# Attention and a rational feed-forward layer: eight of twelve weight conversions moved from the attention's time into the first whole chunk

## The chip, the core and the metric

The kernel runs on one core of a Trainium2 chip. The metric is the device time of one execution in microseconds; lower is better. The engines of the core are PE (matrix products; PEld is its weight load), DVE (vector), ACT (scalar and activation functions), POOL (the third elementwise engine) and SP, whose queue issues almost all DMAs of this kernel. Each engine takes its instructions in the order in which they stand.

## The reference, cut to what matters

```python
def _attn_ref(q, k, v):            # 8 batches, 8 heads, 576 positions, 64 wide
    scores = scale * np.matmul(q, k.transpose(0, 1, 3, 2))
    mask = block_i >= block_j      # blocks of 64 positions
    scores = np.where(mask, scores, -1000000000.0)
    attn = softmax(scores)
    return np.matmul(attn, v)
...
def _moe_ref(x, w_in, w_out, a, b):   # x: 4608 tokens x 512; d_ff = 2048
    h = x @ w_in
    P = a[0] + a[1] * h + a[2] * h2 + a[3] * h3
    Q = 1.0 + np.abs(b[0]) * np.abs(h) + np.abs(b[1]) * h2
    g = P / (Q + 1e-06)
    return g @ w_out
```

The attention's output, heads side by side, is x. The softmax is written out in the reference. The two weight matrices come as 64-bit floats.

## The kernel before, in words

**Precision.** Products are made with pairs of a high and a low part: a matrix product is three matmuls (high with high, high with low, low with high). A weight tile is therefore converted before use: the 64-bit words are put together into a 32-bit float, which is then split into a high part and a remainder.

**Blocks and steps.** d_ff is cut into 16 blocks of 128. Two blocks have four tiles of 128 x 2 x 512: two of w_in and two of w_out. One tile is one conversion step (`Weights.convert`, L142 to L181, a generator that makes a step each time it is asked): a load of 512 KB on SP (L153), an absolute value with scaling on ACT (L164), a shift on DVE (L165), two combined shift-or operations on DVE (L166, L168), a copy to the high part on ACT (L172 or L177), and a subtraction for the low part on POOL (L173 or L178). For the first ten blocks the raw words are loaded into the very tile that later holds the two parts, and the working tile `ab` of the shift lies in PSUM. For the last six blocks, whose weight tiles have no room in SBUF while the attention runs, the step takes its buffers from the rings `os`, `u`, `v` and `s` of the feed-forward units, works in SBUF throughout (`ab` is `at`), and stores the two parts in a scratch tensor in DRAM (L180, two DMAs of 256 KB). These are twelve steps; they are spread over attention steps 80 to 230 (WB0, WBN).

**The attention** takes 32 pairs of heads, ten small steps each: scores (L513, L530), maximum (L548), exponential (L560), division (L569, L572), transposes (L598) and the product with v (L648, L664). A pair's output is split into xh and xl and stored to `xscr`; half of xh is first copied across the partitions by a DMA into xt (L668), added to xl on POOL (L671), and xl is then stored (L672).

**The feed-forward layer** works in units, of two blocks by 256 tokens in the first phase and one block by 512 tokens in the second. A unit has a first product (`first`, L229), whose result h goes through ACT, POOL and DVE (L236 to L245), a reciprocal by logarithm and exponential with a correction (`recip`, L251 to L269), a split into gh and gl (`split`, L277 and L278), and a second product (`second`, L299). The three stages run one, two and three units behind the first. The first phase computes the first ten blocks for 14 chunks of 256 tokens while the attention runs, and stores partial sums to `pscr` (L310). The second phase begins with a whole chunk (chunk 7: all 16 blocks, 16 units, of which the first ten need only the blocks that are there), goes on with seven chunks that add the last six blocks to the partial sums, and ends with another whole chunk. A chunk's x is loaded from `xscr` in four tiles (L214).

**At the change of phase** (L752 to L764) the attention's pools are given back, and the tiles of the last six blocks, the pool `ffb` and further PSUM buffers are opened in their place. Then the rest of the units is emitted in half-steps n = 0, 1, 2 ...; from n = 4 (WF) on, each half-step also issues one reload of a converted tile from the scratch tensor (L761, 512 KB), twelve in all.

A scheduler then sets the order on each engine from the program and its own model of times; the order that is written is not the order that runs.

Of the kernel before, what the change touches and what calls it, by code (L numbers as in the profile page):

```python
# [8 lines left out]
F32 = mybir.dt.float32  # L9
# [24 lines left out]
KQB = 3  # L34
XB = 3
WR, WF = 1, 4
HOLD = 4
ALAG3 = 10
OFFS = (0,3,5)
# [11 lines left out]
NFA = 10  # L51
NFB = NF - NFA
# [8 lines left out]
def units_of(ph, c):  # L61
    return NFA // NBU[0] if ph == 0 else NFB if c < NSP else NF
# [11 lines left out]
def attn_ffn_kernel(  # L74
# [16 lines left out]
    ffn = ctx.enter_context(tc.tile_pool(name="ffn", bufs=2))  # L91
    ps_h = ctx.enter_context(tc.tile_pool(name="ps_h", bufs=1, space=PSUM))
# [27 lines left out]
    class Weights:  # L120
# [19 lines left out]
        def wout(self, f, y):  # L140
            return self.tile(("o", f, 0))[:, y]

        def convert(self):
            last = []
            for key in self.places:
                x, f, d = key
                f += self.f0
                src = w_in[d * 128:(d + 2) * 128, f * 128:(f + 2) * 128] if x == "i" else w_out[f * 128:f * 128 + 128]
                nm = f"{x}{f}_{d}"
                there = self.dt is F32R  # L150
# [7 lines left out]
                                      reason="order")  # L158
                words = raw.rearrange("p a f -> p (a f)").rearrange("p (f t) -> p f t", t=2)
                w0, w1 = words[:, :, 0], words[:, :, 1]  # L160
                at = ffn.tile([128, 512], F32, name=f"wa{nm}", tag="u")
                ab = ps_h.tile([128, 512], F32, name=f"wc{nm}", tag="a") if there else at
                ai, bi = at.bitcast(I32), ab.bitcast(I32)
                nc.scalar.activation(out=ab, in_=w1.bitcast(F32), func=AF.Abs, scale=WSCALE)  # L164
                nc.vector.tensor_scalar(out=bi, in0=bi, scalar1=3, scalar2=None, op0=ALU.logical_shift_left)  # L165
# [8 lines left out]
                else:  # L174
                    bt = ffn.tile([128, 512], F32R, name=f"wb{nm}", tag="v")
                    pt = ffn.tile([128, 512], F32R, name=f"wp{nm}", tag="s")
# [7 lines left out]
    class Ffn:  # L184
# [13 lines left out]
        def load(self, ph, c):  # L198
            n = CTS[ph]
            nd = 512 // n  # L200
            self.x[ph, c] = []
            for i in range(4 // nd):

                pool = self.pools[-1] if ph and (4 * ORDER.index(c) + i + 4) % 6 < 3 else ffn
                if ph and c == ORDER[0] and i == 1:
                    x = ffn.tile([128, nd, 2, n], F32R, name=f"x{ph}_{c}_{i}", tag="os")
                else:
                    x = pool.tile([128, nd, 2, n], F32R, name=f"x{ph}_{c}_{i}", tag="x", bufs=XB)
                t0 = c * n
                while t0 < (c + 1) * n:  # L210
                    b = t0 // S
                    t1 = min((c + 1) * n, (b + 1) * S)
                    for d in range(nd):
                        nc.sync.dma_start(out=x[:, d, :, t0 - c * n:t1 - c * n].bitcast(F32),  # L214
                                          in_=xscr[b][:, nd * i + d, :, t0 - b * S:t1 - b * S])
                    t0 = t1
                self.x[ph, c] += [x[:, d] for d in range(nd)]
# [144 lines left out]
    with ExitStack() as actx:  # L362
# [344 lines left out]
            assert not todo  # L707

        wA = Weights(wpool, 0, NFA, F32R)
        wsteps = wA.convert()  # L710
        load(0)
        for _ in range(C0):
            next(wsteps)
# [3 lines left out]
        ff = Ffn()  # L717
# [10 lines left out]

        KB = NPAIR * 10
        wscr = Weights(dpool, NFA, NFB, F32)  # L730
        wstepsB = wscr.convert()
        NWA, NWB = 2 * NFA, 2 * NFB
        wdone = C0
        WSTEPS = [0] * C0 + [(W0 * (i + 1)) // 4 for i in range(4 - C0)] + [WA + WD * i // 4 for i in range(NWA - 4)]

# [1 line left out]
        there = [((b + 1) * KB + LAST, min(2 * NSP, ((b + 1) * S) // CT)) for b in range(B)]  # L737
        E0, E1, U1 = there[0][0], there[-2][0], there[-2][1] * units_of(0, 0) * 2 - HOLD
        for step in attn_steps():
# [13 lines left out]
    ffb = ctx.enter_context(tc.tile_pool(name="ffb", bufs=2))  # L753
# [1 line left out]
    ff.ready = NCH  # L755
    ps_b = ctx.enter_context(tc.tile_pool(name="ps_b", bufs=1, space=PSUM))
    ff.pools, ff.hpools = [ffn, ffb], [ps_h, ps_b]
    rest = list(wscr.places)
    for n, _ in enumerate(fsteps):
        for key in rest[:WR] if n >= WF else []:  # L760
            nc.sync.dma_start(out=ff.w[1].tile(key).bitcast(F32), in_=wscr.tile(key))  # L761
        if n >= WF:
            rest = rest[WR:]
    assert not rest  # L764


# [28 lines left out]
```

## Time and profile before

| | |
|---|---|
| median of 3 runs | 1247.28 us (1245.51 to 1249.93) |
| the profiled execution | 1246.05 us |
| its span, first to last instruction | 1244.3 us |
| mean granted TensorE clock | 0.994 |
| attention and first phase | about 0 to 822 us |
| second phase | from there to the end |
| DMA traffic | 145.67 MB, 117 GB/s over the span |

The profile is of one execution. Its span leaves out 1.75 us of the execution's own time. Busy time is counted by engine; a matmul's end is modelled, and matmuls follow each other before the one ahead has ended, so small pauses of PE do not show in its busy time. In a timeline row stand the start, the duration, the engine, the line, the operation and the tiles it writes and reads; in brackets stand the idle time ahead of it and what ended that. In the rows of one line stand minimum, median and maximum of its durations in ns.

### The profile page before, as it was taken

How to read it: one execution, taken by the hardware profiler on the slowest of the kernel's cores; microseconds unless marked ns; L12 is line 12 of the kernel's file. 1: busy time of each engine (PE TensorE's matmuls, PEld its weight loads, DVE VectorE, ACT ScalarE, POOL GpSimd, SP SyncE). 2: the span in 40 equal slices, each digit the busy share in tenths (PEclk: the TensorE clock that was granted, in tenths of full speed). 3: DMA queues.
4: the chain of work that ended last, by engine and by line, in shares of the span. 5: the costliest groups of instructions: out<-in, count | busy, mean ns of one | idle time of the engine just before them, and what ended most of it. 6: DMA issues, size and time to landing. Idle time of an engine off the chain costs nothing.

```text
span 1244.3 us, 21931 instructions
## 1 busy us (share of the span) xinstructions
PE 1191.3 (96%) x7124; PEld 1008.8 (81%) x7124; DVE 921.3 (74%) x2016; ACT 908.5 (73%) x2025; POOL 876.7 (70%) x1043
## 2 busy tenths in 40 slices
PE   6888999999999999999999999999999999999998
PEld 4666888888888878888888888878888888888886
DVE  6878888777888777877777777647666766677764
ACT  6877888877988878888888888756555655555554
POOL 4666778877888877787777877756665656665664
PEclk8999999999999999999999999999999999999999
DMA  8782344463544545443333342444014344443100
GB/s 233 208 232 71 94 138 113 121 179 89 143 114 132 132 125 143 108 136 100 100 103 92 105 110 68 113 154 189 1 64 131 120 136 136 136 136 102 43 1 34
DMA packets 199506, 145.67 MB, mean 117 GB/s; under 512 B 136288, under 2 KB 164960, under 8 KB 199392
## 3 DMA queue, kind: packets, MB, share of 16 engines
q1 hardware_dynamic: 196624, 143.15, 40.1%
q10 hardware_dynamic: 2704, 1.11, 0.3%
q8 instruction: 57, 0.93, 0.3%
q14 instruction: 57, 0.47, 0.1%
q0 software_dynamic: 64, 0.00, 0.0%
HBM read 92.28 MB, written 41.94 MB: 108 GB/s over the span
## 4 chain that ended last, share of the span: by engine, by line
PE 71%; ACT 8%; POOL 7%; DVE 5%; DMA 5%; issue 3%; SPq 1%; POOLq 0%; ACTq 0%; DVEq 0%
PE h L229 28%; PE o L299 26%; PE o L664 5%; PE t L598 4%; PE s L530 4%; ACT p L560 2%; PE o L625 2%; POOL gl L275 2%; DMA xt<-xh 1%; POOL u L263 1%; PE tp L438 1%; POOL p L572 1%; PE s L513 1%; DMA wri<-in_moe_w_in_dram 1%; DMA x<-xscr 1%
## 5 line engine op out<-in xcount | busy, mean ns | idle before, releaser
L229 PE MATMUL h<-x,wpi 128*128 128x256 f32 (+1 forms) x2568 | 453.6, 324 | 7.2 <-DMA x<-xscr 2.5
L229 PEld LDWEIGHTS h<-x,wpi 128*128 128x128 f32 x2568 | 380.7, 190 | 53.0 <-issue 6.0
L299 PE MATMUL o<-wpo,gh 128*128 128x512 f32 x1152 | 343.8, 395 | 0.0
L299 PEld LDWEIGHTS o<-wpo,gh 128*128 128x128 f32 x1152 | 212.8, 188 | 43.3 <-issue 0.7
L299 PE MATMUL o<-wpo,gl 128*128 128x512 f32 x576 | 210.3, 400 | 8.6 <-POOL gl L275 8.2
L572 POOL TENSOR_SCALAR p<-p,rc 128x128 f32<-128x128 f32 (+4 forms) x288 | 176.1, 623 | 48.4 <-DVE rc L569 32.9
L243 POOL TENSOR_TENSOR u<-v,u 128x512 f32<-128x512 f32 x144 | 187.5, 1302 | 13.2 <-ACT v L239 5.4
L560 ACT ACTIVATE p<-s,nm 128x288 f32<-128x288 f32 (+4 forms) x320 | 168.3, 534 | 25.2 <-DVE nm L548 19.9
L251 ACT ACTIVATE v<-u,qcb 128x512 f32<-128x512 f32 x144 | 105.1, 730 | 82.0 <-POOL u L243 81.7
L244 DVE TENSOR_TENSOR s<-s,h 128x512 f32<-128x512 f32 x144 | 98.5, 684 | 86.4 <-ACT s L241 65.2
L236 ACT ACTIVATE u<-h 128x512 f32<-128x512 f32 x144 | 86.4, 600 | 102.3 <-PE h L229 96.2
L548 DVE TENSOR_REDUCE nm<-s 128x1 f32<-128x128 f32 (+4 forms) x288 | 129.4, 474 | 7.4 <-PE s L513 4.7
L278 POOL TENSOR_TENSOR gl<-s,gh 128x512 fp32r<-128x512 f32 x74 | 95.8, 1294 | 55.0 <-ACT gh L277 54.9
L598 PE MATMUL t<-ident,p 128*128 128x128 f32 x800 | 122.5, 279 | 8.6 <-POOL p L572 4.1
L299 PEld LDWEIGHTS o<-wpo,gl 128*128 128x128 f32 x576 | 104.7, 189 | 31.1 <-POOL gl L275 12.4
L611 ACT CAST ptrh<-t 128x512 fp32r<-128x512 f32 (+1 forms) x189 | 98.4, 542 | 36.9 <-PE t L598 36.6
L612 DVE TENSOR_TENSOR ptrl<-t,ptrh 128x512 fp32r<-128x512 f32 (+1 forms) x189 | 115.5, 627 | 11.5 <-ACT ptrh L611 10.4
L242 POOL TENSOR_SCALAR v<-u,bab 128x512 f32<-128x512 f32 x74 | 57.2, 774 | 91.0 <-ACT u L236 90.9
L598 PEld LDWEIGHTS t<-ident,p 128*128 128x128 f32 x800 | 91.0, 141 | 27.8 <-POOL p L572 6.8
L263 POOL TENSOR_TENSOR u<-s,u 128x512 f32<-128x512 f32 x70 | 90.3, 1290 | 30.3 <-DVE u L261 16.2
L245 DVE SCALAR_TENSOR_TENSOR s<-s,coef,h 128x512 f32<-128x512 f32 x144 | 106.2, 738 | 2.4
L530 PE MATMUL s<-k,q 64*128 64x512 f32 (+3 forms) x768 | 86.4, 343 | 6.6 <-ACT p L560 2.9
(110 smaller groups left out, 2031.5 us busy)
## 6 DMA issues: line engine op xcount, KB each, us to landing
x<-xscr SPq DMA_DIRECT2D x44, 256.0 KB, 4.0
xscr<-xl SPq DMA_DIRECT2D x32, 288.0 KB, 2.4
out_dram<-os SPq DMA_DIRECT2D x34, 256.0 KB, 3.3
qr<-in_q_dram SPq DMA_DIRECT2D x64, 128.0 KB, 2.8
kr<-in_k_dram SPq DMA_DIRECT2D x62, 128.0 KB, 2.5
xt<-xh SPq DMA_DIRECT2D x54, 144.0 KB, 2.3
xscr<-xh SPq DMA_DIRECT2D x54, 144.0 KB, 2.5
pscr<-os SPq DMA_DIRECT2D x14, 512.0 KB, 2.7
```

What stands on the lines that cost most here:

```text
L229: nc.tensor.matmul(h[:, j, :], lhsT=w.win(f, dc, y), rhs=xs[dc][:, hl, :], start=(dc == 0 and i == 0), stop=(dc == 3 and i == 2))
L243: nc.gpsimd.tensor_tensor(out=ut, in0=vt, in1=ut, op=ALU.mult)
L245: nc.vector.scalar_tensor_tensor(out=st, in0=st, scalar=a1, in1=hf, op0=ALU.add if ph == 0 else ALU.subtract, op1=ALU.mult)
L251: nc.scalar.activation(out=vt, in_=ut, func=AF.Ln, bias=qcb)
L263: nc.gpsimd.tensor_tensor(out=ut, in0=st, in1=ut, op=ALU.subtract)
L299: nc.tensor.matmul(self.o[m], lhsT=g[:, j, ms], rhs=w.wout(f, y), start=(u == 0 and j == 0 and i == 0), stop=(u == nu - 1 and j == NBU[ph] ...
L530: mm = nc.tensor.matmul(s["s", t, h], lhsT=q[hs, x, 128 * t:128 * t + 128], rhs=k[hs, y, 0:128 * (t + 1)], start=(n == 0 and t == i), stop ...
L548: nc.vector.reduce_max(out=nm[:, j:j + 1], in_=s[d, j][:, :w] if i == 4 else s["s", i, j], axis=AX.X, negate=True)
L560: nc.scalar.activation(out=dst, in_=s.pop((d, j2))[:, :w] if i == 4 else s.pop(("s", i, j2)), func=AF.Exp, bias=nm[:, n:n + 1], scale=1.0, ...
L572: nc.gpsimd.tensor_scalar(out=x, in0=x, scalar1=rc[:, j2:j2 + 1], scalar2=1.0, op0=ALU.mult, op1=ALU.mult)
L598: nc.tensor.transpose(ps[:, 128 * x:128 * x + 128], src[:, 128 * kb:128 * kb + 128], ident)
L612: nc.vector.tensor_tensor(out=dl, in0=src, in1=dh.bitcast(F32), op=ALU.subtract)
```

## The change

Only the first four of the twelve conversion steps (NWE = 4, blocks 10 and 11) are still done in the attention's time, stored to DRAM and reloaded. They are spread over the same attention steps 80 to 230. The other eight (blocks 12 to 15) are made by a second generator, on the weight tiles of the last six blocks themselves: the raw words are loaded into the tile, converted, and written back into it as the two parts, with no scratch tensor. One step is asked for at each half-step from n = 6 (WL) on, which is beside the first units of the whole chunk. Their working buffer comes from the pool `ffb`, in the ring `pt` of three buffers, which is otherwise used from the second chunk on for partial sums; `ab` is that same buffer in SBUF. As with the first ten blocks, a raw load waits for the last DVE operation of the step four before (RW = 4).

```diff
@@ -34,6 +34,8 @@
 WR, WF = 1, 4
+WL = 6
+NWE = 4
@@ -140,9 +142,9 @@
-        def convert(self):
+        def convert(self, places, stage=None):
             last = []
-            for key in self.places:
+            for key in places:
@@ -158,8 +160,9 @@
-                at = ffn.tile([128, 512], F32, name=f"wa{nm}", tag="u")
-                ab = ps_h.tile([128, 512], F32, name=f"wc{nm}", tag="a") if there else at
+                at = stage.tile([128, 512], F32, name=f"wa{nm}", tag="pt", bufs=3) if stage else \
+                    ffn.tile([128, 512], F32, name=f"wa{nm}", tag="u")
+                ab = ps_h.tile([128, 512], F32, name=f"wc{nm}", tag="a") if there and not stage else at
@@ -707,7 +710,7 @@
-        wsteps = wA.convert()
+        wsteps = wA.convert(wA.places)
@@ -728,8 +731,8 @@
-        wstepsB = wscr.convert()
-        NWA, NWB = 2 * NFA, 2 * NFB
+        wstepsB = wscr.convert(wscr.places[:NWE])
+        NWA, NWB = 2 * NFA, NWE
@@ -755,13 +758,16 @@
-    rest = list(wscr.places)
+    rest = list(wscr.places[:NWE])
+    late = ff.w[1].convert(wscr.places[NWE:], ffb)
     for n, _ in enumerate(fsteps):
         for key in rest[:WR] if n >= WF else []:
             nc.sync.dma_start(out=ff.w[1].tile(key).bitcast(F32), in_=wscr.tile(key))
         if n >= WF:
             rest = rest[WR:]
-    assert not rest
+        if n >= WL:
+            next(late, None)
+    assert not rest and next(late, None) is None
```

The lines of the changed kernel stand two or three further down (L299 is L302 there, L269 is L272).

The order on each engine changes from the first of the twelve steps on. Three places matter later. The first is PE behind the attention's last matmul (o31_1). In the names, h0_13_4 is the first product of unit 4 of the first phase's chunk 13, o0_13 that chunk's sum, h1_7_1 the first product of unit 1 of the whole chunk, and x1_7_0 to x1_7_3 its x tiles. Before:

```order
L664 MATMUL o31_1_11622<-ptrl_1535,vst_1536 128x64
L299 MATMUL o0_13_0_11761<-wpo0_4_0_1295,gh0_13_2_11754 128x512 x2
L299 MATMUL o0_13_1_11762<-wpo0_4_0_1295,gh0_13_2_11754 128x512 x2
L229 MATMUL h0_13_4_11776<-x0_13_0_11398,wpi0_8_0_1517 128x256 x6
L229 MATMUL h0_13_4_11776<-x0_13_1_11403,wpi0_8_2_1563 128x256 x6
L229 MATMUL h0_13_4_11776<-x0_13_0_11398,wpi0_8_0_1517 128x256 x6
L229 MATMUL h0_13_4_11776<-x0_13_1_11403,wpi0_8_2_1563 128x256 x6
L299 MATMUL o0_13_0_11761<-wpo0_4_0_1295,gl0_13_2_11755 128x512
L299 MATMUL o0_13_1_11762<-wpo0_4_0_1295,gl0_13_2_11755 128x512
L299 MATMUL o0_13_0_11761<-wpo0_5_0_1317,gh0_13_2_11754 128x512 x2
L299 MATMUL o0_13_0_11761<-wpo0_5_0_1317,gl0_13_2_11755 128x512
L299 MATMUL o0_13_1_11762<-wpo0_5_0_1317,gh0_13_2_11754 128x512 x2
```

Seventeen more rows with 35 matmuls of 512 columns follow there until the first that reads x1_7_3. After the change, these are all the rows between the two:

```order
L302 MATMUL o0_13_0_11649<-wpo0_8_0_1594,gh0_13_4_11766 128x512 x2
L302 MATMUL o0_13_1_11650<-wpo0_8_0_1594,gh0_13_4_11766 128x512 x2
L232 MATMUL h1_7_1_11786<-x1_7_0_11730,wpi0_0_0_338 128x512 x3
L232 MATMUL h1_7_1_11786<-x1_7_1_11733,wpi0_0_0_338 128x512 x3
L302 MATMUL o0_13_0_11649<-wpo0_8_0_1594,gl0_13_4_11767 128x512
L302 MATMUL o0_13_1_11650<-wpo0_8_0_1594,gl0_13_4_11767 128x512
L302 MATMUL o0_13_0_11649<-wpo0_9_0_1621,gh0_13_4_11766 128x512 x2
L302 MATMUL o0_13_0_11649<-wpo0_9_0_1621,gl0_13_4_11767 128x512
L302 MATMUL o0_13_1_11650<-wpo0_9_0_1621,gh0_13_4_11766 128x512 x2
L302 MATMUL o0_13_1_11650<-wpo0_9_0_1621,gl0_13_4_11767 128x512
L232 MATMUL h1_7_0_11743<-x1_7_2_11736,wpi0_0_2_540 128x512 x3
L232 MATMUL h1_7_1_11786<-x1_7_2_11736,wpi0_0_2_540 128x512 x3
```

The rest of the first phase now stands ahead of the attention's last matmul, and so does half of the whole chunk's unit 0.

The second place is DVE in the whole chunk, from unit 0's last operation (L269 on s1_7_0) to unit 2's. Before:

```order
L269 SCALAR_TENSOR_TENSOR s1_7_0_11870<-s1_7_0_11870,coef_97,r1_7_0_11923 128x512
L267 SCALAR_TENSOR_TENSOR u1_7_1_11911<-u1_7_1_11911,r1_7_1_11971 128x512
L244 TENSOR_TENSOR s1_7_2_11959<-s1_7_2_11959,h1_7_2_11944 128x512
L268 SCALAR_TENSOR_TENSOR r1_7_1_11971<-u1_7_1_11911,r1_7_1_11971 128x512
L245 SCALAR_TENSOR_TENSOR s1_7_2_11959<-s1_7_2_11959,coef_97,h1_7_2_11944 128x512
L269 SCALAR_TENSOR_TENSOR s1_7_1_11913<-s1_7_1_11913,coef_97,r1_7_1_11971 128x512
L244 TENSOR_TENSOR s1_7_3_12011<-s1_7_3_12011,h1_7_3_11996 128x512
L245 SCALAR_TENSOR_TENSOR s1_7_3_12011<-s1_7_3_12011,coef_97,h1_7_3_11996 128x512
L267 SCALAR_TENSOR_TENSOR u1_7_2_11957<-u1_7_2_11957,r1_7_2_12023 128x512
L268 SCALAR_TENSOR_TENSOR r1_7_2_12023<-u1_7_2_11957,r1_7_2_12023 128x512
L269 SCALAR_TENSOR_TENSOR s1_7_2_11959<-s1_7_2_11959,coef_97,r1_7_2_12023 128x512
```

After (the first half of the stretch; wai12, wai12_2 and wao12 are the working buffers of the first three late steps):

```order
L272 SCALAR_TENSOR_TENSOR s1_7_0_11758<-s1_7_0_11758,coef_97,r1_7_0_11811 128x512
L168 TENSOR_SCALAR wai12_0_11884<-wai12_0_11884 128x512
L270 SCALAR_TENSOR_TENSOR u1_7_1_11799<-u1_7_1_11799,r1_7_1_11859 128x512
L169 SCALAR_TENSOR_TENSOR wai12_0_11884<-wri10_2_0_11882,wai12_0_11884 128x512
L271 SCALAR_TENSOR_TENSOR r1_7_1_11859<-u1_7_1_11799,r1_7_1_11859 128x512
L171 SCALAR_TENSOR_TENSOR wai12_0_11884<-wri10_2_0_11882,wai12_0_11884 128x512
L272 SCALAR_TENSOR_TENSOR s1_7_1_11801<-s1_7_1_11801,coef_97,r1_7_1_11859 128x512
L247 TENSOR_TENSOR s1_7_2_11847<-s1_7_2_11847,h1_7_2_11832 128x512
L168 TENSOR_SCALAR wai12_2_11920<-wai12_2_11920 128x512
L168 TENSOR_SCALAR wao12_0_11954<-wao12_0_11954 128x512
L248 SCALAR_TENSOR_TENSOR s1_7_2_11847<-s1_7_2_11847,coef_97,h1_7_2_11832 128x512
L169 SCALAR_TENSOR_TENSOR wai12_2_11920<-wri10_2_2_11918,wai12_2_11920 128x512
```

Twelve more rows follow until unit 2's L272; in the whole stretch, from unit 0's last operation on, stand 11 operations of units and 13 of conversion steps. The eighth step's last operation stands behind unit 5's last.

The third place is SP behind the store of the attention's last xl. Before, the last x load and then all twelve reloads stand there, with the store of the last partial sum (pscr13) behind them. After:

```order
L675 DMA xscr7_77<-xl31_11450 128x576
L313 DMA pscr13_91<-os0_13_11876 128x1024
L217 DMA x1_7_3_11739<-xscr7_77 128x2x64
L765 DMA wpi10_0_0_11828<-wpi10_0_0_3601 128x1024
L765 DMA wpi10_0_2_11854<-wpi10_0_2_5036 128x1024
L765 DMA wpo10_0_0_11880<-wpo10_0_0_6509 128x1024
L155 DMA wri10_2_0_11882<-in_moe_w_in_dram 128x2x512
L765 DMA wpo10_1_0_11916<-wpo10_1_0_7943 128x1024
L155 DMA wri10_2_2_11918<-in_moe_w_in_dram 128x2x512
L155 DMA wro10_2_0_11952<-in_moe_w_out_dram 128x1024
```

The store of pscr13 has moved ahead of the last x load, and the first raw load (wri10_2_0) stands behind three reloads. Two x loads of the next chunk (x1_0_1 and x1_0_2), which stood just ahead of the store of xl, now stand ahead of the last xt copies.

## The prediction

> **What bounds the kernel now.** I read the page first, then stretches of time with the busy time of each engine, then the rows of the conversion steps, the chain of waits, and the timelines around the end of the attention. Lines are those of the kernel before.
>
> ```profile
> span 1244.3 us, 21931 instructions
> PE 1191.3 (96%) x7124; PEld 1008.8 (81%) x7124; DVE 921.3 (74%) x2016; ACT 908.5 (73%) x2025; POOL 876.7 (70%) x1043
> ```
>
> PE is busy for 96% of the span, so a change gains only what it takes out of PE's idle time, and loses what it adds there. The stretches say where that idle time lies (the columns are the stretch, its length, then the busy time of PE, PEld, DVE, ACT and POOL).
>
> ```profile
> 150.00:560.00 410.00, 393.05 (x2707) 341.75 (x2707) 329.88 (x805) 341.65 (x825) 326.07 (x405) 0.99 0.47 130
> 565.00:800.00 235.00, 232.90 (x1624) 204.93 (x1622) 176.98 (x444) 193.79 (x463) 182.74 (x228) 1.00 0.38 100
> 855.20:882.40 27.20, 27.20 (x121) 22.52 (x120) 17.19 (x26) 14.43 (x25) 15.34 (x14) 1.00 0.00 1
> ```
>
> All twelve conversion steps of the last six blocks run between 152 and about 550 us (rows in part 3). There PE idles 17.0 us of 410 (4.1%); later in the attention, without conversions, 2.1 us of 235 (0.9%). In the whole chunks PE has no idle time, and DVE is busy 17.2 of 27.2 us: five units, since a unit is two groups of 12 matmuls at 2.72 us (below). So eight steps leave a time in which every engine is at about 80% and go to one in which PE alone sets the pace, beside a DVE with 2.0 us to spare in each 5.44 us.
>
> **Part 1: what leaves the attention's time.** The twelve stretches that hold a conversion, and the eleven between them, sum up to:
>
> ```profile
> sum 188.00, PE 175.21 PEld 149.68 DVE 150.06 ACT 156.88 POOL 151.61; mean PE 14.60 PEld 12.47 DVE 12.51 ACT 13.07 POOL 12.63
> sum 224.00, PE 219.84 PEld 194.03 DVE 180.50 ACT 186.53 POOL 174.81; mean PE 19.99 PEld 17.64 DVE 16.41 ACT 16.96 POOL 15.89
> ```
>
> PE is busy 93.2% beside a conversion and 98.1% between them: 0.049 x 188 = 9.3 us for twelve steps, 6.2 us for eight. Against the attention after 565 us it is (4.1% - 0.9%) x 410 = 13.3 us for twelve, 8.9 us for eight. I take **-7.0 us**, nearer to the local comparison. This has the steps' DMAs in it as well: each loads 512 KB and stores two tiles of 256 KB through SP's queue, and each holds one buffer of the units' rings u, v and s, which the units of the first phase then wait for:
>
> ```profile
>   ACT u L236: 4.8, 6
> ```
>
> (that row is from the line of the conversion's subtraction on POOL, and says who waited for it). The eight reloads from the scratch tensor go too, at no gain: they land while PE works on the first ten blocks, which need none of them.
>
> **Part 2: the end of the attention.** With the rings free the scheduler puts first-phase work earlier. Between the attention's last matmul and the first matmul that reads the last x tile of the whole chunk stood 46 matmuls of 512 columns and 24 of 256; now there are 24 of 512. What they covered is a chain of transfers. First PE's timeline, then the chain of waits (start, duration, what):
>
> ```profile
> 821.44 0.28 PE L664 MATMUL o<-ptrl,vst 128*128 128x64 f32 x1
> 822.55 3.04 PE L229 MATMUL h<-x,wpi 128*128 128x256 f32 x24
> 837.61 1.62 PE L229 MATMUL h<-x,wpi 128*128 128x512 f32 x6 [1.36 <-DMA x<-xscr]
> ```
>
> ```profile
> 822.84 5.02 DMA xt<-xh
> 828.03 1.44 POOL xl L671
> 829.48 5.87 DMA xscr<-xl
> 835.40 2.07 DMA x<-xscr
> 868.32 2.72 PE h L229 x12
> ```
>
> From 821.55 to 837.61 are 16.1 us, in which PE had 46 x 0.227 + 2.9 = 13.3 us of work. The 24 matmuls that are left are 5.4 us, and 8 of them (1.8 us) stood behind the chain before, so 13.3 - 3.6 = 9.7 us of work now lie ahead of the attention's last matmul. The chain itself should be shorter. SP's issues and, from the page, the median time from issue to landing of the same transfers:
>
> ```profile
> 822.84 2.02 SPq L668 DMA_DIRECT2D xt<-xh  x1
> 825.61 2.62 SPq L214 DMA_DIRECT2D x<-xscr  x5
> ```
>
> ```profile
> xscr<-xl SPq DMA_DIRECT2D x32, 288.0 KB, 2.4
> xt<-xh SPq DMA_DIRECT2D x54, 144.0 KB, 2.3
> ```
>
> The second xt copy held SP for 2.0 us behind an x load that no longer stands there, and the store of xl took 5.9 us for 2.4 since five x loads were queued ahead of it; two of the three large ones (512 KB) are now issued before the last xh. I take off the 2.0 us and two thirds of the 3.5 us: 16.1 - 4.3 = 11.8 us. The ends are 9.9 us (both transfers at their medians) and 16.1 us. The last x load thus lands 9.7 - 4.3 = **5.4 us** later than before, the gain of part 1 not counted (3.5 to 9.7). The store of the last first-phase chunk now also stands ahead of that load on SP; it waits for ACT's copies of a unit that PE finishes 4 us behind the last attention matmul, so it is issued while xl's store is under way, and I count it at nothing (up to 1.3 us if its 512 KB delay the load).
>
> **Part 3: the steps beside the chunk.** The price of one step, from its rows in the attention's time (min/median/max in ns):
>
> ```profile
> L164 ACT ACTIVATE wai<-sti x6: 677/711/731, 152.6 to 475.2; 128x512 f32<-128x512 f32 x6
> L165 DVE TENSOR_SCALAR wci<-wci x10: 678/700/700, 12.3 to 108.5; 128x512 int32<-128x512 int32 x10
> L165 DVE TENSOR_SCALAR wai<-wai x6: 402/554/1009, 153.9 to 476.6; 128x512 int32<-128x512 int32 x6
> L166 DVE SCALAR_TENSOR_TENSOR wao<-sto,wao x6: 662/712/1129, 224.8 to 546.2; 128x512 int32<-128x512 int32 x6
> L168 DVE SCALAR_TENSOR_TENSOR wao<-sto,wao x6: 664/676/989, 227.0 to 548.1; 128x512 int32<-128x512 int32 x6
> L177 ACT CAST wbi<-wai x6: 618/623/647, 157.7 to 482.1; 128x512 fp32r<-128x512 f32 x6
> L178 POOL TENSOR_TENSOR wpi<-wai,wbi x6: 1282/1512/1824, 158.5 to 482.8; 128x512 fp32r<-128x512 f32 x6
> ```
>
> That is 1.9 to 2.0 us of DVE a step, 1.3 us of ACT and 1.3 to 1.5 us of POOL: 16, 11 and 11 us in all. ACT and POOL have room (14.4 and 15.3 of 27.2 us); DVE has 2.0 us a unit, so eight steps need eight units, and the order packs them into six. On DVE the work of unit 2 counts, since PE waits for its gh:
>
> ```profile
> 844.11 0.69 DVE L268 SCALAR_TENSOR_TENSOR r<-u,r 128x512 f32<-128x512 f32 x1
> 844.84 0.75 DVE L269 SCALAR_TENSOR_TENSOR s<-s,coef,r 128x512 f32<-128x512 f32 x1
> 851.73 0.75 DVE L269 SCALAR_TENSOR_TENSOR s<-s,coef,r 128x512 f32<-128x512 f32 x1
> 853.58 0.62 ACT L277 CAST gh<-s 128x512 fp32r<-128x512 f32 x1
> 857.95 1.98 PE L299 MATMUL o<-wpo,gh 128*128 128x512 f32 x8
> ```
>
> From unit 0's last operation (844.84) to unit 2's (851.73) were 6.9 us. Now 11 operations of units and 13 of steps stand there: 11 x 0.72 + 4 x 1.95 + 0.5 = 16.2 us, so unit 2's comes 9.3 us later. Before, its gh was cast 1.1 us after that operation had ended, and then lay for 3.75 us (854.20 to 857.95) before PE took it. PE therefore takes it 9.3 - 4.9 = **4.4 us** later. From unit 2's last operation to unit 4's stand 11 operations of units and 7 of steps, 11 x 0.72 + 7 x 0.65 = 12.5 us, for which PE has two units, 10.9 us: another **1.6 us**. From there to unit 6's they are 8 and 4, 8.5 us, and DVE catches up. Zero is the other end for both, if PE reaches unit 2 late anyway. The new waits of the raw loads (the fifth to the eighth for the DVE of four steps before) hold up on SP only each other and an x load that is wanted some 50 us later. ACT's first step waits for the fourth transfer behind the last x load:
>
> ```profile
> DMA to landing us min/median/max: 3.9/7.4/10.2
> 835.81 0.94 SPq L761 DMA_DIRECT2D wpi<-wpi  x2
> 843.67 0.72 ACT L251 ACTIVATE v<-u,qcb 128x512 f32<-128x512 f32 x1 [0.39 <-POOL u L243]
> ```
>
> The fourth is issued at about 837.3 on that scale and lands, between 3.9 and 7.4 us later, at 841 to 845; ACT gets there at 844.4. I count it at nothing; being late by its upper end costs about 0.5 us.
>
> **The sum.** -7.0 + 5.4 + 4.4 + 1.6 = +4.4 us. The profiled execution took 1246.05 us (1.75 us of it outside the span), 1.2 us below the median of 1247.28 us of the three runs. I forecast **1250.4 us**, 0.35% above the profiled execution; about 0.3%, or 3.7 us, is also what a measurement of this kernel can tell from no change.
>
> [...] The rows of a step show DVE operations with all operands in SBUF at 402 to 1129 ns, and POOL's subtraction at up to 1824 where its shortest is 1282; the one quoted of the first ten blocks, whose operand lies in PSUM, stays within 678 and 700 ns. [...]
>
> **The rivals.**
>
> 1. *Faster: the backlog is hidden.* If unit 2 is reached late on PE for any other reason, DVE's 6.0 us cost nothing, and the larger relief with the shortest chain gives -8.9 + 3.5 = -5.4: 1240.7 us. For it: over the stretch of five units DVE idles 10.0 of 27.2 us, and PE's second matmuls follow three units behind the first. Against it: the order puts 13 DVE operations of steps ahead of unit 2, whose lead is 3.75 us. It decides when DVE does the 24 operations in under 11.8 us, or PE comes over 4.4 us later. Chance 0.24.
> 2. *Much slower: DVE and POOL block each other.* In the chunk POOL is busy 15.3 of 27.2 us (56%) with operations of up to 1.3 us. If each of the 24 DVE operations of the steps waits half of one at that share, it is 24 x 0.56 x 0.65 = 8.7 us more of DVE work on PE's path: about 1259 us. Against it stand the medians above. Chance 0.10.
> 3. *No change: a trade.* The relief of 7 to 9 us is eaten by the hand-over and part of the backlog: 1246 us. That the attention does not get shorter by the relief, since its own chain bounds it, leads here or higher. Chance 0.16.
>
> **The numbers.** The forecast's case holds 0.50, from +1 to +8 us: 0.35 of it slower by over 0.3%, 0.15 within. With the rivals: faster 0.22 (rival 1, but for 0.02 that stay within 0.3%), same 0.15 + 0.16 + 0.02 = 0.33, slower 0.35 + 0.10 = 0.45. The range goes from rival 1 (1240.7) to the upper ends together (-6.2 + 9.7 + 6.0 + 2.5 us for a third of rival 2's waits = +12.0): 1240.7 to 1258.0 us. The forecast's own case is 1247 to 1254 us.
>
> **What would show it.** PE's idle time between 150 us and the end of the attention falls by 6 to 9 us. Behind the attention's last matmul PE waits 5 us or more for the x load, against 1.4 us. In the first whole chunk, where PE never waited behind unit 0, it waits for gh before the second matmuls of units 0, 2 and 4, and DVE is busy for some 35 us without a gap. L165 shows durations over 1 us there. The prediction is wrong if PE is as dense in that chunk as before, or if the attention's idle time does not fall.

## The result and the profile after

The changed kernel takes 1262.79 us (median of 6 runs, 1261.13 to 1268.08), the kernel before 1246.39 us (6 runs): a ratio of 1.0137, with a 95% interval of 1.0107 to 1.0168. It is 16.4 us slower; the forecast was 4.4 us slower, with a range that ended at 1258.0 us. Lines below are those of the changed kernel, three higher than before in the feed-forward. First the page's head:

```profile
span 1260.7 us, 21891 instructions
PE 1201.8 (95%) x7124; PEld 1016.7 (81%) x7124; DVE 942.2 (75%) x2016; ACT 908.3 (72%) x2025; POOL 871.8 (69%) x1043
```

The same 7124 matmuls keep PE busy 10.5 us longer (1201.8 against 1191.3), and DVE 20.9 us for the same 2016 operations. Both want a reason, since no work was added. The timeline of PE from the attention's last matmul on:

```profile
828.62 0.28 PE L667 MATMUL o<-ptrl,vst 128*128 128x64 f32 x1
...
834.95 1.63 PE L232 MATMUL h<-x,wpi 128*128 128x512 f32 x6 [1.19 <-DMA x<-xscr]
841.48 2.72 PE L232 MATMUL h<-x,wpi 128*128 128x512 f32 x6 [4.90 <-DMA x<-xscr]
845.77 8.64 PE L232 MATMUL h<-x,wpi 128*128 128x512 f32 x24 [1.58 <-DVE s L248]
...
870.01 3.78 PE L302 MATMUL o<-wpo,gh 128*128 128x512 f32 x8 [3.46 <-ACT gh L280]
```

These are the waits of the forecast: for the last x load, and for unit 2's gh. What it had not is how long the matmuls behind them take: 8 in 3.78 us, where 8 took 1.98 before. Stretches of this time (the third number from the end is the granted clock, as a mean over the stretch):

```profile
841.40:851.50 10.10, 8.44 (x20) 6.08 (x21) 6.58 (x10) 6.46 (x11) 5.01 (x5) 0.52 1.00 387
851.50:858.50 7.00, 7.00 (x31) 5.78 (x30) 7.00 (x9) 6.22 (x11) 6.67 (x7) 0.96 0.31 107
866.30:869.90 3.60, 0.24 (x2) 0.00 (x0) 3.60 (x7) 1.57 (x4) 2.24 (x3) 0.88 0.22 31
869.90:875.30 5.40, 5.29 (x13) 4.13 (x14) 5.40 (x8) 4.25 (x8) 5.32 (x5) 0.50 0.20 80
```

Behind both long waits the clock stands at half: it is 0.50 from 841.76 to 852.00 us and from 869.07 to 875.89 us. The 33 matmuls in the first and the last of these rows take 13.7 us, where they would take 7.5 us at 0.227 us each; that is 6.2 of PE's 10.5 us. The rest fits the attention's start: the mean clock of the first 150 us was 0.93 in this execution and 0.98 in that of before. PE's waits in the table of waits, from 820 to 890 us, first of before and then of after:

```profile
PE h L229 <- DMA x<-xscr: 1.4, 1, 1.4
PE o L299 <- POOL gl L275: 0.8, 1, 0.8
PE h L229 <- DVE s L245: 0.4, 1, 0.4
```

```profile
PE h L232 <- DMA x<-xscr: 6.1, 2, 4.9
PE o L302 <- ACT gh L280: 4.2, 2, 3.5
PE h L232 <- DVE s L248: 2.5, 2, 1.6
PE o L302 <- POOL gl L278: 0.5, 1, 0.5
PE h L232 <- DVE xl L670: 0.4, 1, 0.4
```

13.7 us of waits stand for 2.6; 0.5 us of the 13.7, the wait for gl, lie just ahead of the attention's last matmul. Of DVE's 20.9 us, 9.7 are in the eight late steps: they take 26.3 us, and the twelve of the kernel before took 24.9, so eight some 16.6. The four steps in the attention (12.9 us for some 8.3) and the first phase's L264 (69.0 us for 58.8) took longer too. The late steps' operations between 846 and 892 us, by shape (count, then busy us and mean ns of one), and three rows of DVE's and POOL's timelines:

```profile
L169 DVE SCALAR_TENSOR_TENSOR wao<-wro,wao 128x512 int32<-128x512 int32 x4 | 6.7, 1680 | 0.0
L169 DVE SCALAR_TENSOR_TENSOR wai<-wri,wai 128x512 int32<-128x512 int32 x4 | 4.3, 1076 | 0.0
L171 DVE SCALAR_TENSOR_TENSOR wao<-wro,wao 128x512 int32<-128x512 int32 x4 | 4.2, 1047 | 0.0
L171 DVE SCALAR_TENSOR_TENSOR wai<-wri,wai 128x512 int32<-128x512 int32 x4 | 3.8, 951 | 0.0
L168 DVE TENSOR_SCALAR wai<-wai 128x512 int32<-128x512 int32 x4 | 3.8, 942 | 0.0
L168 DVE TENSOR_SCALAR wao<-wao 128x512 int32<-128x512 int32 x4 | 3.5, 884 | 0.0
```

```profile
858.44 1.68 POOL L246 TENSOR_TENSOR u<-v,u 128x512 f32<-128x512 f32 x1
858.89 1.78 DVE L169 SCALAR_TENSOR_TENSOR wao<-wro,wao 128x512 int32<-128x512 int32 x1
861.80 0.68 DVE L171 SCALAR_TENSOR_TENSOR wao<-wro,wao 128x512 int32<-128x512 int32 x1
```

The 24 operations take 26.3 us, 3.3 us a step, where I had counted 1.95. One that starts beside one of POOL's operations on two tiles (L176, L246, L281) ends 0.3 us (L168) or 0.55 us (L169, L171) behind it; there are 13 of these, of 1.2 to 1.8 us. The others take 0.42 us (L168) and 0.68 us. At last the attention, PE's busy time from 150 to 800 us, of before and of after:

```profile
150.00:800.00 650.00, 630.95 (x4370) 551.37 (x4369) 510.32 (x1253) 538.61 (x1294) 510.97 (x635) 0.99 0.44 119
```

```profile
150.00:800.00 650.00, 634.84 (x4403) 558.05 (x4404) 509.39 (x1224) 532.59 (x1279) 494.54 (x626) 0.99 0.40 107
```

PE idles 15.2 us there instead of 19.0. That is 3.9 us of relief in these two profiles, for 7.0. Of the signs that the prediction named one is missing: PE does not wait for gh ahead of unit 0's second matmuls (854.25), only ahead of those of units 2 and 4.

### The profile page after: what moved, and what is told of

It reads as the page before. It is cut to its first block, busy times and chain, and to the rows that moved or that the text cites. A ratio compares the mean times of both kernels' runs of the same rounds, so it can differ in the third digit from the quotient of the medians.

```text
span 1260.7 us, 21891 instructions
## 1 busy us (share of the span) xinstructions
PE 1201.8 (95%) x7124; PEld 1016.7 (81%) x7124; DVE 942.2 (75%) x2016; ACT 908.3 (72%) x2025; POOL 871.8 (69%) x1043
## 4 chain that ended last, share of the span: by engine, by line
PE 75%; DVE 9%; ACT 6%; DMA 3%; issue 3%; POOL 2%; SPq 1%; DVEq 0%; POOLq 0%; ACTq 0%
PE h L232 28%; PE o L302 27%; PE o L667 6%; PE s L533 4%; PE t L601 4%; PE o L628 2%; ACT p L563 2%; PE tp L441 1%; DVE nm L551 1%; PE s L516 1%; DVE ptrl L615 1%; DMA xscr<-xl 1%; DMA wri<-in_moe_w_in_dram 1%; DVE s L247 1%; DVE s L248 1%
## 5 line engine op out<-in xcount | busy, mean ns | idle before, releaser
L232 PE MATMUL h<-x,wpi 128*128 128x256 f32 (+1 forms) x2568 | 460.1, 326 | 14.1 <-DMA x<-xscr 6.5
L302 PE MATMUL o<-wpo,gh 128*128 128x512 f32 x1152 | 347.8, 397 | 4.3 <-ACT gh L280 4.2
L302 PEld LDWEIGHTS o<-wpo,gh 128*128 128x128 f32 x1152 | 213.4, 189 | 48.4 <-ACT gh L280 5.0
L302 PE MATMUL o<-wpo,gl 128*128 128x512 f32 x576 | 213.7, 402 | 4.1 <-POOL gl L278 4.1
L575 POOL TENSOR_SCALAR p<-p,rc 128x128 f32<-128x128 f32 (+4 forms) x288 | 171.3, 606 | 48.9 <-DVE rc L572 36.4
L246 POOL TENSOR_TENSOR u<-v,u 128x512 f32<-128x512 f32 x144 | 187.4, 1301 | 13.6 <-ACT v L242 5.6
L281 POOL TENSOR_TENSOR gl<-s,gh 128x512 fp32r<-128x512 f32 x74 | 97.0, 1312 | 49.6 <-ACT gh L280 49.6
L302 PEld LDWEIGHTS o<-wpo,gl 128*128 128x128 f32 x576 | 105.7, 191 | 26.0 <-POOL gl L278 5.5
L248 DVE SCALAR_TENSOR_TENSOR s<-s,coef,h 128x512 f32<-128x512 f32 x144 | 106.2, 737 | 2.7 <-DVE s L247 0.2
L533 PE MATMUL s<-k,q 64*128 64x512 f32 (+3 forms) x768 | 86.9, 345 | 11.8 <-DVE s L528 4.5
```

What stands on the lines that cost most here:

```text
L232: nc.tensor.matmul(h[:, j, :], lhsT=w.win(f, dc, y), rhs=xs[dc][:, hl, :], start=(dc == 0 and i == 0), stop=(dc == 3 and i == 2))
L246: nc.gpsimd.tensor_tensor(out=ut, in0=vt, in1=ut, op=ALU.mult)
L248: nc.vector.scalar_tensor_tensor(out=st, in0=st, scalar=a1, in1=hf, op0=ALU.add if ph == 0 else ALU.subtract, op1=ALU.mult)
L302: nc.tensor.matmul(self.o[m], lhsT=g[:, j, ms], rhs=w.wout(f, y), start=(u == 0 and j == 0 and i == 0), stop=(u == nu - 1 and j == NBU[ph] ...
L533: mm = nc.tensor.matmul(s["s", t, h], lhsT=q[hs, x, 128 * t:128 * t + 128], rhs=k[hs, y, 0:128 * (t + 1)], start=(n == 0 and t == i), stop ...
L575: nc.gpsimd.tensor_scalar(out=x, in0=x, scalar1=rc[:, j2:j2 + 1], scalar2=1.0, op0=ALU.mult, op1=ALU.mult)
```

## The experiments

Each median stands beside the kernel before on the same chip (1246.0 to 1247.7 us). My theory B: the steps make DVE late, and DVE's backlog ends the chunk's start. Rivals: C, the halved clock is a cost of its own; X, DVE and POOL shut each other out. Theory H: the rest of the loss is the uncovered hand-over. A number behind a median is its ratio to the kernel before on that chip, with the 95% interval. The kernel before itself differs by 1.7 us between the chips, so a difference between two experiments' medians is uncertain by about as much.

**1. Full clock in the wait.** 20 matmuls that nobody reads, in PE's wait for the last x load:

```diff
+if ph and c == ORDER[0] and u == 1 and dc == 3:
+    for i in range(20): nc.tensor.matmul(d, lhsT=w.win(f, 2, 0), rhs=xs[2][:, 0, :], ...)
```

> The changed kernel with 20 matmuls of 512 columns added, whose product nobody reads, right behind the matmuls of unit 1 on the third x tile, that is in PE's wait for the last x load (4.9 us without a matmul in the changed kernel, after which 24 matmuls come 0.43 us apart instead of 0.227, at a granted clock of 0.52). They take 4.5 us. Theory C (the halved clock behind the waits is a cost of its own): the matmuls behind the load run 0.227 us apart, PE is 4 to 5 us ahead, the time is 1258 us (1256 to 1260). Theory B (DVE's backlog sets the end of the chunk, and the slow matmuls only fill time in which PE would wait for gh): the clock stays at 1.0 there, but PE waits the same 4 to 5 us more before unit 2's second matmuls; 1262 us (1260 to 1265).

Measured 1262.27 us, ratio 1.0142 (1.0123 to 1.0160): as the changed kernel. The clock's stretch, and the waits of PE in this kernel:

```profile
841.40:851.50 10.10, 7.71 (x33) 6.05 (x34) 6.93 (x11) 7.26 (x13) 5.09 (x5) 1.00 1.01 382
```

```profile
PE o L307 <- ACT gh L285: 7.4, 3, 4.4
```

The clock is full, and the waits for gh grow from 4.2 to 7.4 us. Theory B stands, C falls for this kernel: the slow matmuls lie under DVE's backlog.

**2. No steps.** The eight late steps left out (so these tiles hold copies of others, and the last blocks' weights are not the reference's):

```diff
-late = ff.w[1].convert(wscr.places[NWE:], ffb)
+nc.sync.dma_start(out=ff.w[1].tile(key)..., in_=wscr.tile(wscr.places[wscr.places.index(key) % NWE]))
```

> The changed kernel without the eight late steps: they are left out, and their tiles are filled with copies of the four steps' tiles in the scratch tensor, by as many reloads as the kernel before has (so the last four blocks of the first phase's partner weights are other weights). Attention and hand-over are as in the changed kernel, the steps' work on DVE, ACT and POOL in the first whole chunk is gone. Theories B and C both: the waits for DVE behind the hand-over go (1.6 + 1.0 + 3.5 + 0.7 us of waits and 2.4 us of slow matmuls behind the second one, 9 us), the wait for the last x load and the slow matmuls behind it stay: 1254 us (1251 to 1257), 5 to 11 us over the kernel before. Rival (the steps are not the cost; the hand-over or the attention is): 1260 us or more. If the hand-over costs nothing either: 1244 us.

Measured 1255.21 us, 1.0071 (1.0054 to 1.0087). The steps cost 7.6 us (7.1 against experiment 1, on the same chip); 9.2 us are left without them. PE's waits from its last attention matmul on, and the slow stretch:

```profile
PE h L232 <- DMA x<-xscr: 6.7, 2, 5.5
PE h L232 <- DVE s L248: 1.6, 1, 1.6
PE h L232 <- DVE xl L670: 0.4, 1, 0.4
```

```profile
845.10:853.00 7.90, 6.28 (x14) 4.50 (x15) 4.21 (x7) 5.03 (x8) 4.07 (x4) 0.50 0.99 391
```

No wait for gh is left; the hand-over's are all there: 8.7 us of waits, and 6.3 us of PE at half clock, which is 3.1 us lost.

**3. Other operations in the steps.** Each step's three operations read one strided word array each (so the floats are not put together):

```diff
+nc.vector.tensor_scalar(out=bi, in0=w1, ...); (out=bi, in0=w0, ...); (out=ai, in0=w1, ...)
```

> The changed kernel with the three DVE operations of each late step replaced by three that read one strided operand from SBUF each (a shift or a mask of one word; the weights of these four blocks are then other numbers, the float is not put together). Their shortest time should be 0.7 us each, 2.0 us a step, no less than the 1.8 us of the originals at their shortest. In the changed kernel 14 of 24 of these operations took 1.2 to 1.8 us and ended with a POOL operation's end, 12 us in all above their shortest. Theory X (DVE and POOL shut each other out): all 24 stay at 0.7 us, DVE's backlog falls by some 10 us, PE's wait for unit 2's gh goes (3.5 us and 2.4 us of slow matmuls behind it): 1255 us (1252 to 1258). Rival (it is the number of operations ahead of unit 2 that counts): the same 1262 us (1260 to 1265).

Measured 1259.66 us, 1.0112 (1.0095 to 1.0129): 3.1 us less, between the two. The operations did not stay short:

```profile
L169 DVE TENSOR_SCALAR wai<-wri 128x512 int32<-128x512 int32 x4 | 5.0, 1255 | 0.0
L171 DVE TENSOR_SCALAR wai<-wri 128x512 int32<-128x512 int32 x4 | 2.2, 540 | 0.0
```

I had expected 0.7 us for each; the six groups of four took 0.53 to 1.26 us in the mean. DVE's time for the steps fell from 26.3 to 19.3 us, but this is no clean test of X; what X costs in time stays open.

**4. One step per unit.** The raw load of each step waits for an earlier unit's last DVE operation:

```diff
+if stage: tc.add_manual_dep(got.ins, ff.rec.ins.name, ...)   # ff.rec: L272 of the unit last emitted
...
-if n >= WL:
+if n >= WL and n % 2 == 0:
```

> The changed kernel with one late step per unit instead of two: each step's raw load waits for the last operation of an earlier unit on DVE, so the steps lie between units 1 and 9 instead of 0 and 5. The work is all done. Theory B: one step of 1.9 to 3 us fits beside a unit's 3.45 us of DVE in 5.44 us or nearly so, and the units lead by three; the waits for gh go, the hand-over's stay: 1254 us (1251 to 1257). If the steps cost DVE more than it has to spare even then (theory X at its strongest, 3.3 us a step): waits of about 1 us in each of eight units, 1258 to 1262 us.

Measured 1259.90 us, 1.0113 (1.0094 to 1.0131); run again twice, 1258.62 us and, in a single run, 1255.66 us. Some 3 to 4 us better than in a bunch, not the 9 hoped for. The time is that of the second case, but its waits of 1 us in each of eight units do not show: PE waits 0.3 to 1.7 us for gh in the profiles of this kernel.

These three profiles also show where the times of one kernel scatter. The attention's last matmul starts at 833.86, 827.50 and 825.11 us, but from there to the end of the whole chunk (DVE's first copy of its sum) it is 112.3, 111.9 and 111.9 us. Measured by this stage, which holds the same matmuls in the changed kernel (117.2 us), here, and without steps (108.0 us), the eight steps cost 9.2 us in a bunch and 4.0 us spread.

**5. Later loads of the next chunk.** Without steps, the three x loads of 512 KB for the next chunk wait until this chunk's last x load has landed:

```diff
+if (ph, c) == (1, ORDER[0]): self.got = got
+elif (ph, c) == (1, ORDER[1]): tc.add_manual_dep(got.ins, self.got.ins.name, ...)
```

> The kernel without the eight late steps, with the three large loads for the next chunk issued only after the last x load of this one has landed: three of 512 KB no longer share the DMA engines with the store of xl (6.0 to 6.5 us there, 2.4 at the median of all 32). Theory H with the store slowed by these loads: store 3 us, last x load 3 us earlier, PE's long wait 2 to 3 us instead of 5.6, and the matmuls behind it not slow: 1250 us (1248 to 1253). Rival (the store is slow for another reason, such as the loads for this chunk or its own small packets): store 5 us or more, 1255 us.

Measured 1249.91 us, 1.0015 (1.0001 to 1.0029): 5.3 us less. The chain of waits, without steps and then with the later loads:

```profile
832.57 2.34 DMA xt<-xh
836.48 6.53 DMA xscr<-xl
843.09 2.01 DMA x<-xscr
```

```profile
831.81 2.29 DMA xt<-xh
835.71 3.86 DMA xscr<-xl
839.58 2.01 DMA x<-xscr
```

The store takes 2.7 us less, the other links of the chain are as they were. Theory H holds for this half: the store of xl was slow because of those loads. The stage from the attention's last matmul to the end of the chunk is 2.6 us shorter (105.4 for 108.0); where the rest of the 5.3 us went is not shown, and the kernel before was 1.7 us slower on this chip, not faster.

**6. Full clock without a backlog.** As 1, in the kernel without steps:

```diff
+    for i in range(22): nc.tensor.matmul(d, lhsT=w.win(f, 2, 0), rhs=xs[2][:, 0, :], ...)
```

> The kernel without the eight late steps, with 22 matmuls of 512 columns that nobody reads in PE's wait for the last x load (5.0 us of 5.6). In the changed kernel the like brought nothing, since DVE's backlog ended later than the slow matmuls. Here there is no backlog. If the halved clock is a cost of its own without a backlog: the 11 slow matmuls and the slow ones in the gaps go, 2.5 to 4 us: 1252 us (1250.5 to 1253.5). If the refill (two units that finish at once, behind one bank of PSUM) sets the pace anyway: 1255 us (1254 to 1257).

Measured 1252.45 us, 1.0039 (1.0024 to 1.0054): 2.8 us less, 2.1 us of it in the stage behind the attention (105.9 for 108.0), and the clock is 1.00 where it was 0.50. Where no backlog covers it, the halved clock does cost.

**7. First-phase work tied behind the attention.** Without steps:

```diff
+if (ph, c) == (0, 2 * NSP - 1) and u in (3, 4): tc.add_manual_dep(mm.ins, ff.last.ins.name, ...)   # last attention matmul
```

> The kernel without the eight late steps, with the first matmuls of the last two units of the first phase tied behind the attention's last matmul, so that the scheduler can't put them ahead: by the order 8.6 us of matmuls stand in the hand-over before the first one on the last x tile instead of 5.4, and 5 us more that need no x tile stand behind its first three. Theory H (what the kernel without steps loses to the kernel before, 9 us, is the uncovered wait and what follows it): the chain stays at 12 to 13 us, the wait is 3 to 4 us instead of 7, the refill behind it is covered by the 5 us, no matmul behind it is slow: 1249 us (1247 to 1252). Rival (attention and total are set elsewhere; work moved out of the attention leaves idle time there): 1255 us (1253 to 1258).

Measured 1254.67 us, 1.0049 (1.0032 to 1.0066): no gain, a miss. The stretch from 750 us to the last attention matmul, without steps and then with the tie:

```profile
750.00:831.60 81.60, 79.58 (x548) 69.91 (x546) 63.07 (x154) 65.28 (x157) 60.45 (x81) 1.00 0.33 88
```

```profile
750.00:827.50 77.50, 72.73 (x473) 62.58 (x472) 55.82 (x140) 56.35 (x143) 53.68 (x74) 0.96 0.30 79
```

The waits behind the attention fell from 8.7 to 5.2 us and the clock stayed up, but PE idles 4.8 us ahead of it instead of 2.0, at a clock of 0.96 for 1.00. Those matmuls had filled gaps of the attention; what covers the hand-over is missing there. Behind the attention 3.5 us of waits and the 3.1 us of slow matmuls are gone; ahead of its end 2.8 us of idle time and about 3 us by the lower clock have come in their place.

**8. Holding back the first phase** (HOLD 12 for 4): without steps, in the kernel before, and with all twelve steps left out.

```diff
-WR, WF = 1, 4
+WR, WF = 1, 12
-HOLD = 4
+HOLD = 12
```

> The kernel without the eight late steps (tiles filled with copies, as before), and the first phase of the feed-forward held back by eight more half-steps (HOLD 12 for 4, and the reloads begin eight half-steps later, so at the same unit of the whole chunk): by the order, 8.3 us of matmuls stand between the attention's last matmul and the first one on the last x tile instead of 5.4, and two of the three large loads of the next chunk stand behind the store of xl instead of ahead of it. Theory H (the 9 us that the kernel without steps loses to the kernel before are the hand-over: an uncovered wait of 7 us, the slow matmuls behind it and the refill): PE's wait falls to 2 to 4 us in pieces, no matmul behind it is slow; 1248 us (1245 to 1251). Rival (the attention itself has become slower by its new order): 1255 us (1253 to 1258).

> The kernel before with the same holding back (HOLD 12, reloads eight half-steps later). By the order, 8.3 us of matmuls stand in the hand-over instead of 13.3. Theory H: its hand-over was covered already, so there is nothing to gain; with a chain of 12 us, as in the changed kernel, up to 3.5 us become uncovered: 1248 us (1244 to 1252). If holding back helps by itself, in the attention and not in the hand-over: 1242 us or less.

> As the kernel without late steps and with HOLD 12, and the last four steps are left out of the attention too (all twelve tiles are then filled with copies of tiles of the first ten blocks). It tells what conversions cost the attention. Theory R (PE idles beside them, 0.5 to 0.7 us a step by the prediction): 2 to 3 us faster than the kernel with four steps and the same hold. Theory Z (the idle time has other owners, and goes elsewhere with each new order): the same within 2 us, either way.

Measured 1254.89 us (1.0069; 1.0052 to 1.0085), 1265.20 us (1.0149; 1.0128 to 1.0169) and 1254.06 us (1.0060; 1.0043 to 1.0077). The first two miss: holding back gains nothing and costs the kernel before 18 us (PE idles 25.3 us between 150 and 800 us there, for 19.0). The last says that four steps more or less in the attention are worth 0.8 us. That is theory Z's case, but by the two intervals it is uncertain by about 3 us, so theory R's 2 to 3 us are not excluded.

**9. The later loads with all the work done:** in the changed kernel, in the kernel before, and with one step per unit two units later (between units 4 and 11). The edit is that of 5, and for the third kernel that of 4 with

```diff
-WL = 6
+WL = 10
```

> The changed kernel, all eight steps as they are, with the next chunk's three large loads issued only after the last x load has landed. Without the steps this took 5 us. If hand-over and steps add up (H and B, in a row): the x load lands 3 us earlier, the steps' raw loads too, and DVE's backlog as a whole begins 3 us earlier: 1259 us (1257 to 1261). If the backlog swallows it, as it swallowed the full clock: 1262 us (1261 to 1264).

> The kernel before with the same later loads. By its order 10.5 us of matmuls cover the hand-over instead of 13.3. Its waits there were 3.5 us in all. If a chain that is 2 to 3 us shorter is a gain by itself: 1244 us. If cover and chain shrink together: 1247 us (1245 to 1249), no change.

> One step per unit as in the spread kernel, but two units later (between units 4 and 11), behind the refill of the hand-over, and the next chunk's loads later too. All the work is done. If the steps are free once they stand beside units that lead by three: 1251 us (1249 to 1252.5), the 1250 us of the kernel without steps and with the same loads. If eight steps cost 3 to 4 us there as well (as in the first spread kernel: waits for gh of unit 2, and one of 1.4 us later): 1254 us (1252.5 to 1256).

Measured 1258.46 us (1.0094; 1.0076 to 1.0111), 1244.99 us (0.9983; 0.9971 to 0.9995) and 1255.61 us (1.0062; 1.0047 to 1.0076). The first comes as the adding theory had it. The second lies nearest to the "gain by itself", at the border of the other case; the kernel before with later loads is the only version that beats both, by 2.2 us, and its interval stays just below 1. The third comes in its second case, though dearer than 3 to 4 us: the steps are not free, 5.7 us above the kernel without steps. ACT's timeline there shows a wait that the edit itself brought in:

```profile
892.70 0.66 ACT L171 ACTIVATE wai<-wri 128x512 f32<-128x512 f32 x1 [0.92 <-DMA wri<-in_moe_w_in_dram]
...
895.27 0.68 ACT L171 ACTIVATE wai<-wri 128x512 f32<-128x512 f32 x1 [0.76 <-DMA wri<-in_moe_w_in_dram]
895.85 0.71 ACT L264 ACTIVATE v<-u,qcb 128x512 f32<-128x512 f32 x1
```

With 12 unread matmuls in the wait as well:

> The same with 12 matmuls of 512 columns that nobody reads (2.7 us) in PE's wait for the last x load, which is 3 us there. If the halved clock is a cost where no backlog stands behind it (2.8 us for 22 of them in the kernel without steps): 1.5 to 2.5 us less, 1249 us (1247 to 1251). If the shorter wait no longer halves the clock: the same as without them, 1251 us.

Measured 1256.82 us (1.0078; 1.0060 to 1.0095): no gain, a miss. In the stage behind the attention it is 1.1 us less (109.4 for 110.5), which the scatter of the attention hides.

**10. Raw loads early, the steps still spread.** ACT's first operation of a step waits for the unit, not the load:

```diff
-if there and len(last) >= RW:
+if there and not stage and len(last) >= RW:    # no wait for the step four before
...
-    tc.add_manual_dep(got.ins, ff.rec.ins.name, ...)
+    tc.add_manual_dep(go.ins, ff.rec.ins.name, ...)   # go: L167
```

> As the kernel with one step per unit between units 4 and 11 and the later loads for the next chunk, but it is ACT's first operation of a step that waits for an earlier unit's last DVE operation, and not the raw load: the eight raw loads go out at once behind the reloads. In the kernel before this one ACT stood 0.8 to 1.5 us before a step's first operation for its raw load, with the units' operations queued behind it. If those waits are what is left of the steps' price: 1251 us (1249 to 1253), as without steps. If DVE and POOL shutting each other out is what is left: 1255 us (1253.5 to 1257).

Measured 1253.36 us, 1.0051 (1.0028 to 1.0074): 2.3 us less, 3.4 us above the kernel without steps, at the edge of the second case. The steps' 24 DVE operations still take 25.7 us there, the largest groups:

```profile
L175 DVE SCALAR_TENSOR_TENSOR wao<-wro,wao 128x512 int32<-128x512 int32 x4 | 6.1, 1536 | 0.1
L175 DVE SCALAR_TENSOR_TENSOR wai<-wri,wai 128x512 int32<-128x512 int32 x4 | 5.2, 1289 | 0.1
L173 DVE SCALAR_TENSOR_TENSOR wai<-wri,wai 128x512 int32<-128x512 int32 x4 | 5.0, 1260 | 0.0
```

3.2 us a step beside a unit's 3.45 us of DVE is 6.7 us in 5.44 us of PE: even spread, a step does not fit beside a unit.

## Why the prediction was wrong, step by step

The direction and the places were right; the size was not. By its terms (forecast, measured):

- **Relief of the attention: -7.0, about -2.2 us.** This step failed most clearly. I took the difference between stretches with and without a conversion (93.2% against 98.1% busy) for the conversion's price. The thirteen profiles of kernels with four steps in the attention, HOLD 4 and no tie idle 15.2 to 17.1 us between 150 and 800 us, 16.1 in the mean; the two with twelve (before, and before with later loads) 19.0 and 17.5. Even 2.2 us may be too much: in that stretch the clock stood at half for 10.5 us in the mean of the thirteen and for 6.8 us in each of the two, which by my estimate, half of the difference, gives 1.8 us back. Leaving four more out gave 0.8 us, within the noise. So most of the idle time beside the conversions was not their price; that it belonged to the attention's own waits and comes up elsewhere in the new order fits this, but no run takes the eight steps out of the attention and changes nothing else.
- **Hand-over: +5.4, some +11.4 us** (9.2 us without steps, plus the 2.2 us of relief). Its wait came out: 1.4 + 5.4 = 6.8 us forecast, 6.1 measured. The chain was 12.9 us (828.62 to 841.48) for 11.8. But the store of xl did not become faster, as I had reckoned; it took 6.0 us, where it took 5.9 before, and the loads that make it slow can be moved (experiment 5). What the step lacked is what follows the wait: the half clock (3.1 us without steps) and 1.6 us of waiting for DVE's L248, which gives a unit's bank of PSUM back, since two units come at once. Waits and clock make 8.7 - 2.6 + 3.1 = 9.2 of the 11.4 us. The other 2 are not located; they go if the relief was as small as the clock suggests.
- **Counting moved work as lost cover** was too simple as well. Experiments 7 and 8 give cover back and gain nothing in the whole, since the attention loses what the hand-over gains (experiment 7). Why the kernel before has enough in both places stays open.
- **Steps beside the chunk: +6.0, +7.6 us.** Mechanism and place were right: PE waits 3.5 us for unit 2's gh (4.4 forecast) and 0.7 for unit 4's (1.6). But between the last operations of units 0 and 2 on DVE lie 19.5 us (849.08 to 868.57), not 16.2, since a step takes 3.3 us of DVE. That PE's wait still came out near the forecast is luck: PE was later at unit 2 too, behind the slow matmuls and the wait for L248.
- **Rival 2** (DVE and POOL block each other), which had 0.10, took place, as far as the 13 long DVE operations that end behind POOL's show it: 26.3 us less the shortest durations (8 x 0.41 + 16 x 0.68 = 14.2) are 12.1 us, even more than its 8.7. It came together with the forecast's case, not in its stead, and part of it was hidden; its share of the 7.6 us is not separated (experiment 3). For the upper end of the range I took a third of the 8.7 as 2.5 us; it is 2.9. I judged by the medians of the attention's steps; of their 36 DVE operations in the kernel before only 11 (540 to 1304 ns) end 0.28 or 0.55 us behind one of POOL's, of the late steps' 24 the 13 long ones above.
- **Nothing** in the sum stood for the clock; in the stretches that the prediction shows it was 0.99 to 1.00. After the waits of 4.9 and 3.5 us it stood at half for 10.2 and 6.8 us (841.76 to 852.00 and 869.07 to 875.89 us), three and two times 3.41 us, and the last stretch of 3.41 us was work without a pause both times. In the whole kernel it cost nothing by itself (experiment 1: a ratio of 1.0142 at full clock, 1.0137 in the changed kernel).

## What to carry to other kernels

A share of idle time beside some work is not the price of that work: leave it out and look before counting on it. Work that moves next to the engine that sets the pace is priced there, beside the engines that run there (here POOL: 3.3 us a step on DVE for 1.95), and not by its rows in a slacker place. A forecast of a long wait of PE has to price the matmuls behind it too (here 33 took 13.7 us for 7.5), and then ask whether another engine's backlog hides them.

## What the runs showed of the hardware

- The clock did not go by the length of one wait. In the profiles of the kernels before and after, its 7 and 17 changes lie whole multiples of 3.41 us apart. Behind the attention in the changed kernel, PE idles 1.8 us of the 3.41 us from 834.93 us, and the next 3.41 us run at full clock; it idles 3.1 us of those from 838.35 us and 2.5 us of those from 865.65 us, and the next run at half. Without steps and with later loads, PE is busy for 0.83 us of one stretch (a wait of 2.89 us lies in it), and the next one runs at half clock:

```profile
839.15:842.56 3.41, 0.83 (x4) 0.73 (x5) 0.00 (x0) 0.00 (x0) 0.00 (x0) 1.00 0.62 149
842.56:845.97 3.41, 1.81 (x5) 0.99 (x4) 1.94 (x3) 2.94 (x5) 2.48 (x3) 0.50 1.02 406
```

In experiment 7 a wait of 3.29 us falls on two stretches, with 1.9 and 1.4 us of idle time, and the clock stays up:

```profile
837.06:840.47 3.41, 1.55 (x10) 1.02 (x8) 1.53 (x3) 1.97 (x3) 2.00 (x2) 1.00 0.77 268
840.47:843.89 3.42, 2.00 (x9) 1.71 (x10) 0.01 (x1) 1.75 (x3) 2.10 (x3) 1.00 0.79 236
```

- A store of 288 KB took 6.5 us beside large loads and 3.9 us without those of the next chunk (experiment 5).
